# Router compares in one operation, splits moved to VectorE, first conversions and router loads moved ahead

## The chip, the cores and the metric

The kernel runs on one core of a Trainium2 chip. The core has a matrix engine (TensorE, PE in the profile, with its weight loads as PEld), VectorE (DVE), ScalarE (ACT), GpSimd (POOL) and SyncE (SP), whose queue issues the DMA transfers of this kernel. The metric is the device time of one execution in microseconds; the median of three runs is compared.

## The reference

Three layers in a row, on 2304 tokens (4 batches of 576), all in float32. Only the third one's routing is unusual: it assigns greedily over all token and expert pairs in the order of their logits, and each expert takes at most 288 tokens.

```python
# 1: block-causal attention, 4 batches x 8 heads x 576 tokens x 64
attn = softmax(where(block_i >= block_j, q @ k.T / sqrt(64), -1e9)) @ v
x = attn.transpose(0, 2, 1, 3).reshape(2304, 512)
# 2: gated feed-forward, 512 -> 1536 -> 512
h = sigmoid(x @ w_gate) * (x @ w_val)
x = h @ w_out
# 3: 8 experts, capacity 2304 // 8 = 288
logits = x @ m_gate
for idx in argsort(-logits.flatten()):
    tok, e = idx // 8, idx % 8
    if assigned[tok] >= 0 or counts[e] >= 288: continue
    assigned[tok] = e; counts[e] += 1
out[assigned == e] = maximum(x[assigned == e] @ w1[e], 0) @ w2[e]
```

## The kernel before

Matrix products keep float32 accuracy by splitting: a tensor x becomes a high part h (a rounded copy, made by ScalarE) and a low part l = x - h (made by GpSimd or VectorE), and a product is the sum of three matmuls, hh, hl and lh. Tiles whose names end in h and l are such parts.

The stages are interleaved by Python generators. Each `yield` hands over to the stage beside it, so the order of the calls of `next` is the order of the instructions on every engine, and each engine works through its own in that order. TensorE is in order too: a matmul that waits holds all behind it.

*Attention and first feed-forward* (`first_half`). Attention runs one batch ahead of the feed-forward. Before its first batch, `Ffn.start` loads the first gate and value weights, which come as 64-bit floats, converts them (`convert`, `ToF32`: one ScalarE operation, L283, and four on VectorE, L288 to L294) and splits them. `first_half` advances it once after each step of attention, from attention's fourth step on. SyncE issues loads in program order; attention's are L70 and L71, the weights' L331.

*Router weights* (`router_weights`) are worked out beside batch 1: w_out is loaded (L529), converted and multiplied with the router's gate. The first step of that generator sets tiles to zero on GpSimd, loads the gate and three tiles of w_out, and starts the first conversion.

*Second feed-forward and router.* `Ffn2.run` computes h @ w_out token tile by token tile, 18 tiles of 128 tokens: 36 matmuls of 512 columns (L660) a tile, and for the last two tiles two times 36 of 256 columns. A step of it is one wide matmul, or on average one and a half narrow ones. It is the filling work for the router. `Ffn2.split` makes the parts of the next tile of h, three chunks of 512: ScalarE L633, then GpSimd L637, then the load of the tile two on. It is advanced after every third matmul.

`Router.run` finds the greedy assignment in seven phases. A phase takes each free token's best expert (`pick`), turns that logit into an ordered key in two halves of 16 bits (`keys`), and searches for each expert's threshold in two halves of three rounds. In a round all keys are compared with 31, 63 or 64 thresholds, 18 matmuls count (L809), VectorE gives the verdict whether an expert is full (`ge`, L816), a flag matmul (L819) turns the verdicts into the new base, and VectorE compares again (L825, L830). The differences of key and threshold are made ahead by `minus` (L796), two a phase on VectorE (558 elements) and two on GpSimd (1134 and 1152), so that a round's compare needs the base alone. At a phase's end the chosen tokens get their logits lowered, and GpSimd adds them to the result (L857, L858). `FILL` says how many steps of `Ffn2.run` stand between the parts of a phase: for each half and round, ahead of the 18 matmuls and ahead of the flag matmul, and a last number ahead of the phase's last matmuls. `FIRST` and `TAIL` do so at the start and end of the router. Five tiles of expert weights are split on GpSimd meanwhile, one step of `Experts.split` with every 18 steps. After the router, `Experts.gather` fetches each expert's tokens by index.

Of the kernel before, what the change touches and what calls it, by code (L numbers as in the profile page):

```python
# [8 lines left out]
F32 = mybir.dt.float32  # L9
# [287 lines left out]
class Ffn:  # L297
# [88 lines left out]
    def start(self):  # L386

        for f in range(2):
            for j in range(2):
                self.load(0, f, j)  # L390
                yield
        for _ in range(3):
            yield
        for f in range(2):
            for j in range(2):
                for _ in self.convert(f, j):
                    yield
        for j in range(2):
            for _ in self.split(0, 0, j):
                yield  # L400
# [112 lines left out]
def router_weights(k, ffn):  # L513
# [36 lines left out]
    raws = [load(f) for f in range(3)]  # L550
    later = iter(())
# [31 lines left out]
class Ffn2:  # L583
# [40 lines left out]
    def split(self, t):  # L624
# [7 lines left out]
        for c in range(3):  # L632
            nc.scalar.activation(h[:, 4 * c:4 * c + 4], x[:, 4 * c:4 * c + 4], AF.Copy)  # L633
            yield
        for c in range(3):
            s = slice(4 * c, 4 * c + 4)
            nc.gpsimd.tensor_tensor(l[:, s], x[:, s], f32(h[:, s]), op=OP.subtract)  # L637
            yield
        self.load(t + 2)
# [8 lines left out]
    def run(self):  # L648

        k, nc = self.k, self.k.nc  # L650
        nxt = iter(())
        order = [(t, 0, 512) for t in range(16)] + [(t, c, c + 256) for c in (0, 256) for t in (16, 17)]
        for i, (t, a, b) in enumerate(order):
            h, l = self.parts[t]
            if a == 0:
                nxt = self.split(t + 1)
            o = k.psF.tile([P, 512], F32, name="A")
            for f in range(12):
                for n, (x, w) in enumerate(((h, self.oh), (h, self.ol), (l, self.oh))):
                    nc.tensor.matmul(o[:, 0:b - a], x[:, f], w[:, f, a:b], start=(f == 0 and n == 0), stop=(f == 11 and n == 2))  # L660
                    if n == 2:
                        next(nxt, None)
                    if b - a == 512 or n == 1 or f % 2:
                        yield
            drain(nxt)
# [15 lines left out]
FILL = (((13, 6), (4, 3), (6, 3)), ((8, 3), (4, 3), (6, 3)), 10)  # L681
# [4 lines left out]
class Router:  # L686
# [4 lines left out]
    def open(self, st, k):  # L691
# [63 lines left out]
        self.sub = [None, t([P, 18 * 31], F32, "sub1"), t([P, 18 * 64], F32, "sub2")]  # L755
# [35 lines left out]
    def minus(self, h, s):  # L791

        J = SEARCH[h][s][1]
        x = self.kf[:, 0 if h == 0 else 2]
        eng = self.k.nc.vector if s == 1 else self.k.nc.gpsimd
        eng.tensor_tensor(self.sub[s][:, 0:18 * J].rearrange("p (c j) -> p c j", j=J),  # L796
                                       x[:, :, None].to_broadcast([P, 18, J]),
                                       self.step[h, s][:, None, :].to_broadcast([P, 18, J]), op=OP.subtract)

    def phase(self, last):  # L800
        nc, k = self.k.nc, self.k
        v, q = nc.vector, self.q
        for h in range(2):
            base = k.psA.tile([P, 512], F32, name="A")
            for s, (sh, J) in enumerate(SEARCH[h]):
# [17 lines left out]
                if s < 2:  # L823
                    J1 = SEARCH[h][s + 1][1]
                    v.tensor_scalar(self.cmp[:, 0:18 * J1], self.sub[s + 1][:, 0:18 * J1], base[:, 0:1], None, op0=OP.is_ge)  # L825
                elif h == 0:
                    v.tensor_scalar(q[:, 0], self.kf[:, 0], base[:, 0:1], 1.0, op0=OP.subtract, op1=OP.min)
                    v.scalar_tensor_tensor(self.kf[:, 2], q[:, 0], 65536.0, self.kf[:, 1], op0=OP.mult, op1=OP.add)
                    J1 = SEARCH[1][0][1]
                    v.tensor_tensor(self.cmp[:, 0:18 * J1].rearrange("p (c j) -> p c j", j=J1),  # L830
                                    self.kf[:, 2, :, None].to_broadcast([P, 18, J1]),
                                    self.step[1, 0][:, None, :].to_broadcast([P, 18, J1]), op=OP.is_ge)

# [21 lines left out]
        if not last:  # L855
            self.pick()
# [3 lines left out]
    def run(self):  # L860
# [5 lines left out]
        for ph in range(7):  # L866
            yield from self.phase(ph == 6)
# [24 lines left out]
        hi = self.sub[1][:, 0:432].rearrange("p (c h) -> p c h", h=24)  # L892
# [22 lines left out]
class Experts:  # L915
# [27 lines left out]
    def split(self, eng):  # L943
# [16 lines left out]
        self.load()  # L960

# [155 lines left out]
def first_half(k, s1, ffn, f2, right):  # L1117
# [4 lines left out]
    while s1.done < 3:  # L1122
        next(att, None)
        if s1.step > 2:
            next(w0, None)
# [3 lines left out]
    for b in range(nb):  # L1129
# [12 lines left out]
        for c in ffn.batch(b, inline):  # L1142
# [4 lines left out]
            if b == 1:  # L1147
# [19 lines left out]
def tile_fn(ctx, tc, q, kk, v, w_gate, w_val, w_out, m_gate, w1, w2, out, dbg=None):  # L1167
# [49 lines left out]
    esp = (x for _ in range(5) for x in ex.split("g"))  # L1217
    with tc.manual_schedule():
        n = 0
# [47 lines left out]
```

## Time and profile before

| | us |
|---|---|
| median of 3 runs | 1002.01 (1000.61 to 1003.71) |
| the profiled execution | 1003.31 |
| its span, first to last instruction | 1001.5 |
| TensorE busy | 955.7 (95%) |
| VectorE busy | 552.7 (55%) |
| GpSimd busy | 475.2 (47%) |
| ScalarE busy | 425.7 (43%) |

The span is what the trace covers, and all its times count from the span's start. A busy TensorE is not a TensorE at its peak, since matmuls are pipelined and its clock has two levels. Where an engine is named after an arrow in a row, the idle time in front of the row ended when that engine's operation did. By stage: attention alone until about 75 us, feed-forward with attention until 440, feed-forward alone until 553, second feed-forward with router until 761, experts to the end.

### The profile page before, as it was taken

To read this page: it belongs to the slowest core of one execution; us is meant where nothing else is said; L and a number is where in the kernel's file an instruction comes from. 1 tells how busy PE (TensorE), PEld (TensorE's weight loads), DVE (VectorE), ACT (ScalarE), POOL (GpSimd) and SP (SyncE) were. 2 spreads that over 40 slices of the span, in tenths; PEclk is the share of its full clock that TensorE was granted. 3 is DMA by queue.
4 is the path that set the end of the run, shared out by engine and by line. 5 is a ranking of instruction groups with operands and counts; after the bars stand their busy time and mean duration, and the time that the engine had idled before them with its cause. 6 is when DMAs were issued, how large, how long until landed. Compare 5 with 4: busy or idle time off the path is not lost.

```text
span 1001.5 us, 19572 instructions
## 1 busy us (share of the span) xinstructions
PE 955.7 (95%) x7387; PEld 824.4 (82%) x7387; DVE 552.7 (55%) x1293; ACT 425.7 (43%) x998; POOL 475.2 (47%) x514
## 2 busy tenths in 40 slices
PE   6899999999999999999999988999998999999996
PEld 4568888879888988889898766666678999999996
DVE  4888888567666444441332476766651544454440
ACT  4676655445555354532431222211111555555551
POOL 2475434433434344362432777866633545445532
PEclk9899999999999999999999999999999999999998
DMA  6664667464554322225782845444323566666640
GB/s 162 173 149 133 200 190 210 132 205 167 172 176 142 111 79 90 72 83 182 263 298 84 224 124 150 142 126 113 106 85 96 189 202 188 198 202 204 199 153 24
DMA packets 191326, 155.17 MB, mean 155 GB/s; under 512 B 70785, under 2 KB 161921, under 8 KB 191233
## 3 DMA queue, kind: packets, MB, share of 16 engines
q1 hardware_dynamic: 187728, 142.92, 47.4%
q0 software_dynamic: 3504, 11.01, 3.2%
q8 instruction: 58, 0.95, 0.4%
q14 instruction: 36, 0.29, 0.1%
HBM read 116.15 MB, written 37.75 MB: 154 GB/s over the span
## 4 chain that ended last, share of the span: by engine, by line
PE 82%; DVE 10%; issue 3%; DMA 2%; POOL 1%; SPq 1%; ACT 1%; DVEq 0%; POOLq 0%; ACTq 0%
PE A L454 31%; PE A L1046 10%; PE A L1091 9%; PE A L660 9%; PE A L211 5%; PE A L163 4%; PE A L116 4%; DVE cmp L825 3%; PE A L809 2%; DVE sub L796 2%; PE A L122 2%; PE A L409 1%; PE A L85 1%; PE A L996 1%; PE A L1015 1%
## 5 line engine op out<-in xcount | busy, mean ns | idle before, releaser
L151 POOL TENSOR_SCALAR p<-p,stat 128x128 f32<-128x128 f32 (+2 forms) x144 | 80.6, 572 | 195.5 <-DVE stat L149 149.7
L454 PE MATMUL A<-xh,w1h 128*128 128x288 f32 x384 | 121.7, 317 | 2.0 <-ACT ptb L168 2.0
L454 PE MATMUL A<-xh,w0h 128*128 128x288 f32 x384 | 121.5, 316 | 0.0
L359 POOL TENSOR_TENSOR w0l<-wf,w0h 128x512 fp32r<-128x512 f32 x48 | 64.0, 1333 | 107.4 <-ACT w0h L357 104.6
L454 PE MATMUL A<-xl,w1h 128*128 128x288 f32 x384 | 113.7, 296 | 0.0
L454 PE MATMUL A<-xh,w1l 128*128 128x288 f32 x384 | 113.7, 296 | 0.0
L454 PE MATMUL A<-xl,w0h 128*128 128x288 f32 x384 | 113.2, 295 | 0.0
L454 PE MATMUL A<-xh,w0l 128*128 128x288 f32 x384 | 113.1, 295 | 0.0
L958 POOL TENSOR_TENSOR ewl<-eraw,ewh 128x512 fp32r<-128x512 f32 x56 | 74.7, 1353 | 68.2 <-ACT ewh L954 68.0
L465 DVE SCALAR_TENSOR_TENSOR h<-sg,A 128x288 f32<-128x288 f32 x96 | 43.3, 451 | 97.0 <-PE A L454 79.8
L124 DVE TENSOR_REDUCE stat<-A 128x1 f32<-128x128 f32 (+4 forms) x160 | 70.5, 478 | 46.7 <-PE A L122 28.4
L660 PE MATMUL A<-wo_h,hl 128*128 128x512 f32 (+1 forms) x240 | 94.5, 394 | 0.4 <-POOL hl L637 0.4
L464 ACT ACTIVATE sg<-A 128x288 f32<-128x288 f32 x96 | 39.3, 410 | 127.5 <-PE A L454 123.2
L660 PE MATMUL A<-wo_l,hh 128*128 128x512 f32 (+1 forms) x240 | 91.8, 383 | 0.0
L660 PE MATMUL A<-wo_h,hh 128*128 128x512 f32 (+1 forms) x240 | 90.3, 376 | 0.0
L138 ACT ACTIVATE p<-A,stat 128x128 f32<-128x128 f32 (+4 forms) x160 | 81.9, 520 | 16.1 <-DVE stat L124 13.1
L637 POOL TENSOR_TENSOR hl<-hraw,hh 128x512 fp32r<-128x512 f32 x54 | 76.1, 1437 | 22.6 <-ACT hh L633 21.6
L454 PEld LDWEIGHTS A<-xh,w1h 128*128 128x128 f32 x384 | 72.6, 189 | 10.5 <-issue 6.5
L667 ACT ACTIVATE x2r<-A 128x512 f32<-128x512 f32 (+1 forms) x20 | 11.1, 556 | 165.0 <-PE A L660 165.0
L454 PEld LDWEIGHTS A<-xh,w0h 128*128 128x128 f32 x384 | 72.3, 188 | 9.2 <-issue 5.2
L1091 PE MATMUL A<-eh,ewh 128*128 128x288 f32 x256 | 78.0, 305 | 0.0
L1046 PE MATMUL A<-exh,ewh 128*128 128x288 f32 x256 | 77.4, 302 | 0.3 <-ACT exh L999 0.3
(223 smaller groups left out, 2602.3 us busy)
## 6 DMA issues: line engine op xcount, KB each, us to landing
eraw<-in_moe_w_dram SPq DMA_DIRECT2D x64, 512.0 KB, 4.4
wf<-wgv SPq DMA_DIRECT2D x72, 256.0 KB, 3.2
h<-h SPq DMA_DIRECT2D x48, 288.0 KB, 2.4
hraw<-h SPq DMA_DIRECT2D x16, 768.0 KB, 5.8
w<-in_moe_w_gate_dram SPq DMA_DIRECT2D x12, 512.0 KB, 3.9
w<-in_moe_w_val_dram SPq DMA_DIRECT2D x12, 512.0 KB, 4.1
wgv<-wf SPq DMA_DIRECT2D x24, 256.0 KB, 3.0
w<-in_moe_w_out_dram SPq DMA_DIRECT2D x12, 512.0 KB, 4.1
```

Source lines behind the costliest of these rows:

```text
L124: nc.vector.tensor_reduce(st[:, x:x + 1], s[:, 0:w], axis=AX.X, op=OP.max, negate=True)
L138: nc.scalar.activation(o, s[:, 0:w], AF.Exp, bias=m, scale=1.0, accum_out=st[:, 2 + x:3 + x])
L151: self.k.mark = nc.gpsimd.tensor_scalar(t, t, r[:, x:x + 1], 1.0, op0=OP.mult, op1=OP.mult)
L211: nc.tensor.matmul(o[64 * a:64 * a + 64, b0:w], vs[0:kk, c, a, :], th[0:kk, a, c, b0:w], start=(n == 0), stop=(n == len(mm) - 1))
L359: nc.gpsimd.tensor_tensor(l, x, f32(h), op=OP.subtract)
L454: nc.tensor.matmul(o[:, 0:288], w[:, ks], x[:, ts], start=(kk == 0 and n == 0), stop=(kk == 3 and n == 2))
L465: nc.vector.scalar_tensor_tensor(h[:, ts], sg, 1.0, ps[1][:, 0:288], op0=OP.add, op1=OP.mult)
L637: nc.gpsimd.tensor_tensor(l[:, s], x[:, s], f32(h[:, s]), op=OP.subtract)
L660: nc.tensor.matmul(o[:, 0:b - a], x[:, f], w[:, f, a:b], start=(f == 0 and n == 0), stop=(f == 11 and n == 2))
L958: (nc.vector if eng == "v" else nc.gpsimd).tensor_tensor(l[:, s], x[:, s], f32(h[:, s]), op=OP.subtract)
L1046: nc.tensor.matmul(o[:, 0:288], w[:, s], x, start=(d == 0 and n == 0), stop=(d == 3 and n == 2))
L1091: nc.tensor.matmul(o[:, 0:288], w[:, s], x, start=(n == 0), stop=(n == 23))
```

## The change

1. *Compare in one operation.* `minus` and its tiles are gone. `at_least` subtracts the base from the key and compares the difference with the thresholds, in one VectorE operation with two tensor inputs.
2. *Splits on VectorE.* The low parts of h (54 operations) and of the first five tiles of expert weights (10) go from GpSimd to VectorE. `aside` places one of them: nine times a phase, ahead of and behind the verdict, and where the tile's three are done, it advances the expert weights (`first_splits`). What is left of a tile's splits when the tile ends is issued there. ScalarE's three copies are issued together at the tile's start.
3. *Sums on VectorE.* The two GpSimd operations at a phase's end become `closed`, in the next phase's third round.
4. *FILL.* A phase has 80 steps in place of 72.
5. *First conversions.* `Ffn.start` is advanced from attention's first step on, and its loads are spread: two behind the fifth load of attention, two behind the eighth.
6. *Router loads.* `router_weights` gives way once behind its loads, and is advanced once at step 180 (of 192) of batch 0.

```diff
@@ Ffn.start
         for f in range(2):
             for j in range(2):
                 self.load(0, f, j)
+            for _ in range((6, 3)[f]):
                 yield
-        for _ in range(3):
-            yield
@@ router_weights
     raws = [load(f) for f in range(3)]
+    yield
@@ Ffn2.split
             nc.scalar.activation(h[:, 4 * c:4 * c + 4], x[:, 4 * c:4 * c + 4], AF.Copy)
-            yield
+        yield
         for c in range(3):
             s = slice(4 * c, 4 * c + 4)
-            nc.gpsimd.tensor_tensor(l[:, s], x[:, s], f32(h[:, s]), op=OP.subtract)
+            nc.vector.tensor_tensor(l[:, s], x[:, s], f32(h[:, s]), op=OP.subtract)
+            if c == 2:
+                self.load(t + 2)
             yield
-        self.load(t + 2)
+
+    def aside(self):
+
+        if next(self.nxt, 1):
+            next(self.more, None)
...
-FILL = (((13, 6), (4, 3), (6, 3)), ((8, 3), (4, 3), (6, 3)), 10)
+FILL = (((14, 4), (5, 3), (9, 3)), ((8, 3), (5, 3), (9, 3)), 11)
@@ Router
-    def minus(self, h, s):
+    def at_least(self, h, s, x, base=0.0):
...
+        self.k.nc.vector.scalar_tensor_tensor(
+            self.cmp[:, 0:18 * J].rearrange("p (c j) -> p c j", j=J), x[:, :, None].to_broadcast([P, 18, J]), base,
+            self.step[h, s][:, None, :].to_broadcast([P, 18, J]), op0=OP.subtract, op1=OP.is_ge)
+
+    def closed(self):
+
+        v = self.k.nc.vector
+        sel = self.q[:, 4][:, None, :].to_broadcast([P, 8, 18])
+        v.tensor_tensor(self.t2, sel, self.e1[:, :, None].to_broadcast([P, 8, 18]), op=OP.mult)
+        v.tensor_tensor(self.res, self.res, self.t2, op=OP.add)
...
                 if h + s == 0:
                     self.keys()
-                if s == 0:
-                    self.minus(h, 1)
-                    self.minus(h, 2)
+                elif (h, s) != (0, 2):
+                    aside()
+                elif not first:
+                    self.closed()
                 v.tensor_scalar(self.ge[0:J], o[0:J, 0:8], CAP - 0.5, 0.0, op0=OP.is_ge, op1=OP.max,
                                 accum_out=self.fl[0:J])
+                if (h, s) != (1, 2):
+                    aside()
                 yield FILL[h][s][1]
...
                 if s < 2:
-                    J1 = SEARCH[h][s + 1][1]
-                    v.tensor_scalar(self.cmp[:, 0:18 * J1], self.sub[s + 1][:, 0:18 * J1], base[:, 0:1], None, op0=OP.is_ge)
+                    self.at_least(h, s + 1, self.kf[:, 2 * h], base[:, 0:1])
...
-        nc.gpsimd.tensor_tensor(self.t2, sel, ex, op=OP.mult)
-        nc.gpsimd.tensor_tensor(self.res, self.res, self.t2, op=OP.add)
@@ Experts
+    def first_splits(self, n):
+        cur = self.split("v")
+        next(cur)
+        yield
+        for i in range(n):
+            next(cur)
+            yield
+            nxt = self.split("v") if i < n - 1 else cur
+            if nxt is not cur:
+                next(nxt)
+            next(cur)
+            next(cur, None)
+            yield
+            cur = nxt
@@ first_half
         next(att, None)
-        if s1.step > 2:
-            next(w0, None)
+        next(w0, None)
...
-            if b == 1:
+            if b == 1 or (b, n) == (0, 180):
                 next(rw, None)
@@ tile_fn
-    esp = (x for _ in range(5) for x in ex.split("g"))
+    f2.more = ex.first_splits(5)
...
-        for w in ro.run():
+        for w in ro.run(f2.aside):
             for _ in range(w):
                 next(steps, None)
-                n += 1
-                if n % 18 == 0:
-                    next(esp, None)
         drain(steps)
-        drain(esp)
+        drain(f2.more)
```

How the instructions move. VectorE, in a phase of the router, from the last key operation to the third verdict, before (`sub` is the difference of key and threshold, `A` a PSUM bank with counts or base):

```order
L789 CAST kf<-ki 128x18
L796 TENSOR_TENSOR sub_7196<-kf,step_7147 128x558
L816 TENSOR_SCALAR ge,flag<-A 31x8
L825 TENSOR_SCALAR cmp<-sub_7196,A 128x558
L816 TENSOR_SCALAR ge,flag<-A 31x8
L825 TENSOR_SCALAR cmp<-sub_7197,A 128x1134
L816 TENSOR_SCALAR ge,flag<-A 63x8
```

The same place of the changed kernel, in a phase where the asides go to a tile of h (`hl` is the low part of h):

```order
L794 CAST kf<-ki 128x18
L827 TENSOR_SCALAR ge,flag<-A 31x8
L637 TENSOR_TENSOR hl_8387<-hraw,hh_8386 128x512
L799 SCALAR_TENSOR_TENSOR cmp<-kf,A,step_7144 128x558
L637 TENSOR_TENSOR hl_8387<-hraw,hh_8386 128x512
L827 TENSOR_SCALAR ge,flag<-A 31x8
L637 TENSOR_TENSOR hl_8387<-hraw,hh_8386 128x512
L799 SCALAR_TENSOR_TENSOR cmp<-kf,A,step_7149 128x1134
L807 TENSOR_TENSOR u_7201<-q_7204,e_7202 128x144
L808 TENSOR_TENSOR res<-res,u_7201 128x144
L827 TENSOR_SCALAR ge,flag<-A 63x8
```

The subtraction ahead of the first verdict is gone; two splits stand around the second verdict, one behind the first, and the two sums ahead of the third.

SyncE at the start, from the fifth load of attention on, before (`raw` holds q or k, `vraw` v, `w` the feed-forward's weights):

```order
L70 DMA raw<-in_k_dram 128x4x64 x2
L71 DMA raw<-in_k_dram 64x2x64
L70 DMA vraw<-in_v_dram 128x4x64 x2
L71 DMA vraw<-in_v_dram 64x2x64
L70 DMA raw<-in_q_dram 128x4x64 x2
L71 DMA raw<-in_q_dram 64x2x64
```

And of the change:

```order
L70 DMA raw<-in_k_dram 128x4x64 x2
L71 DMA raw<-in_k_dram 64x2x64
L331 DMA w_182<-in_moe_w_gate_dram 128x4x256
L331 DMA w_184<-in_moe_w_val_dram 128x4x256
L70 DMA vraw<-in_v_dram 128x4x64 x2
L71 DMA vraw<-in_v_dram 64x2x64
```

The first two weight loads stand behind five loads of attention instead of eleven.

SyncE at the turn from batch 0 to batch 1, the difference (`h_57` is batch 0's h in DRAM, `mg` the router's gate):

```order
-L319 DMA h_57<-h 128x576 x2
-L522 DMA mg<-in_moe_w_gate_dram 128x4x8
-L529 DMA w_2767<-in_moe_w_out_dram 128x1024
-L529 DMA w_2769<-in_moe_w_out_dram 128x1024
-L529 DMA w_2771<-in_moe_w_out_dram 128x1024
+L319 DMA h_57<-h 128x576
+L521 DMA mg<-in_moe_w_gate_dram 128x4x8
+L528 DMA w_2708<-in_moe_w_out_dram 128x1024
+L528 DMA w_2710<-in_moe_w_out_dram 128x1024
+L528 DMA w_2712<-in_moe_w_out_dram 128x1024
+L319 DMA h_57<-h 128x576
```

The four loads stand ahead of the last store of batch 0.

## Rows read from the trace of the kernel before

**Rows 1.** The page: busy us of each engine, share of the span, instructions.

```profile
PE 955.7 (95%) x7387; PEld 824.4 (82%) x7387; DVE 552.7 (55%) x1293; ACT 425.7 (43%) x998; POOL 475.2 (47%) x514
```

**Rows 2.** Timeline, 20.9 to 27 us: start, us, engine, operation [idle before <-releaser].

```profile
20.95 0.59 SPq L331 DMA_DIRECT2D w<-in_moe_w_gate_dram  x1
...
25.35 0.69 ACT L283 ACTIVATE cv_t<-w 128x512 f32<-128x512 f32 x1 [3.50 <-DMA w<-in_moe_w_gate_dram]
...
26.58 0.34 PE L163 MATMUL A<-ident,p 128*64 128x128 f32 x1 [1.85 <-ACT ptb L168]
```

**Rows 3.** Stretches at the lower clock: busy us by engine, PEclk, DMA.

```profile
26.60:33.50 6.90, 6.79 (x25) 2.88 (x27) 6.07 (x16) 5.11 (x16) 3.27 (x7) 0.51 0.57 178
207.50:211.00 3.50, 3.45 (x14) 3.45 (x15) 2.16 (x3) 1.76 (x7) 1.52 (x1) 0.52 0.59 226
651.40:654.80 3.40, 3.40 (x19) 2.49 (x16) 1.65 (x3) 0.00 (x0) 3.20 (x3) 0.51 0.52 155
```

**Rows 4.** Timeline, 193.5 to 208 us.

```profile
193.84 7.33 SPq L319 DMA_DIRECT2D h<-h  x2
...
205.94 0.67 ACT L283 ACTIVATE cv_t<-w 128x512 f32<-128x512 f32 x1 [6.31 <-DMA w<-in_moe_w_out_dram]
...
207.55 0.58 PE L454 MATMUL A<-xh,w1h 128*128 128x288 f32 x1 [2.04 <-ACT ptb L168]
```

**Rows 5.** Chain that ended last: start, us, what; the same operation, two phases.

```profile
688.20 1.52 DVE cmp L825
...
712.01 1.51 DVE cmp L825
```

**Rows 6.** Timeline, 601.8 to 606 us, a phase of the router.

```profile
602.02 0.52 DVE L825 TENSOR_SCALAR cmp<-sub,A 128x558 bf16<-128x558 f32 x1 [0.25 <-PE A L819]
...
602.63 0.40 PE L660 MATMUL A<-wo_l,hh 128*128 128x512 f32 x1
...
602.87 0.61 PE L809 MATMUL A<-oneh,cmp 128*128 128x8 bf16 x18
...
603.51 0.15 DVE L816 TENSOR_SCALAR_CACHE_REDUCE ge<-A 31x8 bf16<-31x8 f32 x1 [0.97 <-PE A L809]
...
604.12 0.18 PE L819 MATMUL A<-flag,wgt 128*128 128x1 bf16 x1
...
604.42 1.24 DVE L825 TENSOR_SCALAR cmp<-sub,A 128x1152 bf16<-128x1152 f32 x1 [0.75 <-PE A L819]
...
604.70 0.40 PE L660 MATMUL A<-wo_l,hh 128*128 128x512 f32 x1
...
605.40 0.40 PE L660 MATMUL A<-wo_l,hh 128*128 128x512 f32 x1
...
605.72 0.43 PE L809 MATMUL A<-oneh,cmp 128*128 128x8 bf16 x11
```

**Rows 7.** Timeline, 694 to 699 us, a later phase.

```profile
694.71 0.74 DVE L830 TENSOR_TENSOR cmp<-kf,step 128x558 bf16<-128x558 f32 x1
...
694.82 2.61 POOL L796 TENSOR_TENSOR sub<-kf,step 128x1152 f32<-128x1152 f32 x1 [1.00 <-DVE kf L828]
...
695.37 2.66 DVE L796 TENSOR_TENSOR sub<-kf,step 128x558 f32<-128x558 f32 x1
```

**Rows 8.** VectorE by line and shape, 565 to 745: busy us, mean ns.

```profile
L825 DVE TENSOR_SCALAR cmp<-sub,A 128x558 bf16<-128x558 f32 x14 | 18.7, 1334 | 7.0 <-PE A L819 7.0
```

**Rows 9.** Whole span by line and shape: busy us, mean ns, idle before.

```profile
L637 POOL TENSOR_TENSOR hl<-hraw,hh 128x512 fp32r<-128x512 f32 x54 | 76.1, 1437 | 22.6 <-ACT hh L633 21.6 <-PE A L819 0.9
...
L574 DVE TENSOR_TENSOR wol<-A,woh 128x512 fp32r<-128x512 f32 x12 | 8.3, 692 | 9.5 <-ACT woh L572 9.3
```

**Rows 10.** Timeline, 742 to 745.5 us, the router's end.

```profile
744.87 0.32 PE L905 MATMUL A<-cmp,ohlo 128*128 128x48 bf16 x6 [1.62 <-DVE ohlo L900]
```

**Rows 11.** Timeline, 755 to 763 us, the first gathers.

```profile
756.06 1.20 POOL L984 DMA_INDIRECT xg<-x2h,idx  x1 [8.86 <-DMA x2h<-x2r]
...
762.85 0.33 PE L996 MATMUL A<-ident,xg 128*128 128x128 f32 x1 [1.04 <-DMA xg<-x2h,idx]
```

More of the change, by code (lines that the diff above doesn't have):

```diff
@@ L650, in run @@
         k, nc = self.k, self.k.nc
-        nxt = iter(())
+        self.nxt = iter(())
         order = [(t, 0, 512) for t in range(16)] + [(t, c, c + 256) for c in (0, 256) for t in (16, 17)]
@@ L655, in run @@
             if a == 0:
-                nxt = self.split(t + 1)
+                self.nxt = self.split(t + 1)
+                next(self.nxt, None)
             o = k.psF.tile([P, 512], F32, name="A")
@@ L660, in run @@
                     nc.tensor.matmul(o[:, 0:b - a], x[:, f], w[:, f, a:b], start=(f == 0 and n == 0), stop=(f == 11 and n == 2))
-                    if n == 2:
-                        next(nxt, None)
                     if b - a == 512 or n == 1 or f % 2:
                         yield
-            drain(nxt)
+            drain(self.nxt)
             y = self.hb.tile([P, 512], F32, name="x2r", bufs=3)
@@ L754, in open @@
         nc.gpsimd.memset(self.cmp, 0.0)
-        self.sub = [None, t([P, 18 * 31], F32, "sub1"), t([P, 18 * 64], F32, "sub2")]
+        self.hot = t([P, 18 * 24], F32, "hot")
         self.ki = t([P, 4, 18], I32, "ki")
@@ L789, in keys, with phase @@
         v.tensor_copy(kf[:, 1], ki[:, 3])
-    def minus(self, h, s):
+    def at_least(self, h, s, x, base=0.0):
         J = SEARCH[h][s][1]
[L794 to L800, printed above, removed]
+        self.k.nc.vector.scalar_tensor_tensor(
[6 more added lines that the diff above has]
+        v.tensor_tensor(self.res, self.res, self.t2, op=OP.add)
+    def phase(self, first, aside):
         nc, k = self.k.nc, self.k
@@ L828, in phase @@
                     v.scalar_tensor_tensor(self.kf[:, 2], q[:, 0], 65536.0, self.kf[:, 1], op0=OP.mult, op1=OP.add)
[L829 to L832, printed above, removed]
+                    self.at_least(1, 0, self.kf[:, 2])
         v.scalar_tensor_tensor(self.e1, o[:, 16:24], 16.0, self.w8, op0=OP.mult, op1=OP.add)
@@ L854, in phase, with run @@
         v.scalar_tensor_tensor(k.L, sel, -BIG, k.L, op0=OP.mult, op1=OP.add)
-        if not last:
-            self.pick()
-        nc.gpsimd.tensor_tensor(self.t2, sel, ex, op=OP.mult)
-        nc.gpsimd.tensor_tensor(self.res, self.res, self.t2, op=OP.add)
-    def run(self):
+    def run(self, aside):
         nc, k = self.k.nc, self.k
@@ L866, in run @@
         for ph in range(7):
-            yield from self.phase(ph == 6)
+            if ph:
+                self.pick()
+            yield from self.phase(ph == 0, aside)
+        self.closed()
         v.tensor_scalar(self.t1, k.L, -0.1 * BIG, None, op0=OP.is_gt)
@@ L891, in run @@
         lo = self.p.tile([P, 18, P], BF16, name="ohlo")
-        hi = self.sub[1][:, 0:432].rearrange("p (c h) -> p c h", h=24)
+        hi = self.hot.rearrange("p (c h) -> p c h", h=24)
         mv = self.cmp[:, 0:864].rearrange("p (c a h) -> p c a h", a=2, h=24)
@@ L1216, in tile_fn @@
             ro.open(rst, k)
-    esp = (x for _ in range(5) for x in ex.split("g"))
+    f2.more = ex.first_splits(5)
     with tc.manual_schedule():
-        n = 0
         with tc.issue_after(k.rowed.ins):
             next(steps)
-        for w in ro.run():
+        for w in ro.run(f2.aside):
             for _ in range(w):
                 next(steps, None)
-                n += 1
-                if n % 18 == 0:
-                    next(esp, None)
         drain(steps)
-        drain(esp)
+        drain(f2.more)
     if dbg is not None:
```

## The prediction

> **What bounds the kernel now.** I read the page's busy times first, then the list of what TensorE (PE) waits for, then the chain that ended last, and then the timeline at each place where PE stood still. PE is busy for 95% of the span [rows 1], and every other engine has slack, so the time is PE's work plus PE's waits plus the stretches at the lower clock. Three places hold nearly all of it that the change touches.
>
> *The start.* SyncE issues the eleven loads of q, k and v one after the other, and the first load of FFN weights leaves only at 20.95 us. ScalarE's first conversion stands ahead of a copy that PE needs. It waits 3.50 us for that load, and PE stands 1.85 us [rows 2]. Right behind, the granted clock is 0.51 for 6.9 us [rows 3], which is the 1.2 GHz level.
>
> *The turn from batch 0 to batch 1.* SyncE holds the last store of h until h is there, from 193.84 on, for 7.33 us with the store before it, and the router's load of w_out stands behind it. ScalarE waits 6.31 us for that load with a copy for PE queued behind, and PE stands 2.04 us [rows 4]; then 3.5 us at clock 0.52 [rows 3].
>
> *The router.* One phase takes 23.81 us, by two rows one phase apart [rows 5]. What must PE do in it? A step of filling work (one matmul of 512 columns) is 0.23 us: three of them lie between 604.70 and 605.40. Between 602.63 and 604.70 lie six steps, one block of 18 compare matmuls (L809) and one flag matmul (L819), with no wait worth counting: 2.07 - 6 x 0.233 = 0.67 us for a block and its flag [rows 6]. Six of them are 4.0, with 0.2 (an estimate) for the three small matmuls at a phase's end. With 72 steps (the sums of FILL) a phase needs 72 x 0.233 + 4.2 = 21.0 us; 2.8 of 23.81 are waits, 19.6 in seven phases. Why it waits is in [rows 7]: GpSimd's subtraction takes 2.61 us, and VectorE's own one beside it takes 2.66 and holds the verdict (L816) behind it. The compare of 558 elements takes 1.33 us on average [rows 8], but 0.52 where GpSimd does not read [rows 6].
>
> **The change, part by part.**
>
> *Compare in one operation.* Both subtractions go (two on VectorE, two on GpSimd a phase), and four compares become one operation with two tensor inputs. The trace has none of that form. The nearest row is the compare of two tensors at L830, 558 elements in 0.74 us [rows 7]; beside the split of 512 in 0.69 [rows 9] that is 1.1 ns an element, so 1.39 us for 1152. I take these. Bounds: 0.52, the old form alone, below, and 1.33 for 558 (its mean today) above. On VectorE the form matters: the Trainium skill, "VectorE: DVE Perf Modes", section "Mode 2×_2P", says that an fp32 operation with one tensor in SBUF can run two elements a cycle and one with two tensors cannot, which speaks against this edit. The trace agrees in part: 0.52 against 0.74 for 558, but 1152 took 1.24 in the old form, no double rate [rows 6]. By that rule alone the two short compares grow by 0.22 us each and cost about 3 us in seven phases if PE waits for them. By the mean of their row today they shrink by 0.59 [rows 8]. The sum goes by the durations of the rows and by the walk below.
>
> *GpSimd leaves the router stage.* Its 54 splits of h, 10 of expert weights and the two sums a phase go to VectorE. A split costs 0.69 on VectorE against 1.44 on GpSimd [rows 9]; 0.69 is from a row with one input in PSUM, and I take it, with 1.44 as the upper bound.
>
> *Do the splits fit?* The walk, with the latencies of [rows 6]: the verdict can start 0.64 us after its block (602.87 to 603.51) and takes 0.15; the flag matmul comes 1.25 after the block with three steps between; 0.30 later a compare can start; 0.06 after its end the next block can. So between the end of one compare and the start of the next VectorE has 0.06 + 1.25 + 0.30 = 1.61 us, and two splits and the verdict need 1.53. They fit, with nothing to spare. After the flag matmul the chain is 0.30 + 0.74 + 0.06 = 1.10 us against 5 steps (1.17), and 0.30 + 1.39 + 0.06 = 1.75 against 9 (2.10). What misses: in two phases a tile of h ends outside the gaps and its remaining splits stand in a row (ahead of the key operations, or of a verdict), 0.6 us late each. I leave 2.0 us of waits in seven phases, between 0.5 and 10 (10 with the compare at 1.33).
>
> *FILL.* 72 steps a phase become 80. The work only moves: the 56 steps no longer stand behind the router. A phase without waits is 80 x 0.233 + 4.2 = 22.8 us. **Router: 19.6 - 2.0 = 17.6 us gained.** The drop to 0.51 at 651.4 [rows 3] lies in this stage; without the waits ahead of it I count it gone, 3.4 x 0.5 = 1.7.
>
> *Costs around the router.* The first three splits of h stand on VectorE behind the last gate of the batch: 0.4 (estimate; bounds 0 and 2, three splits at 0.69). The router's end: PE waits up to 1.62 us there today for the one-hot rows [rows 10]; the same 35 steps now cover half-width matmuls, some 1.7 us less, and three splits (2.1) stand ahead of the chain, while GpSimd no longer disturbs VectorE. 0.6 worse (bounds: 1.6 better, 3.5 worse). Behind the router 35 instead of 91 steps are left, about 6 us. The index goes through gathers from 756.06 to PE's 762.85, 6.8 us, which today wait for the x2 store and not for the index, with 1.04 us of wait left on PE [rows 11]; now both come together: 0.4 worse.
>
> *First conversions sooner.* Weight loads follow the fifth load of attention, so the first leaves near 10 us instead of 20.95, and lands near 14.4 at the same 4.4 us. In ScalarE's order the conversion now stands ahead of the first copy of transposed probabilities, for which I estimate 16 us. The 1.85 us go; of the 6.9 us at 0.51, which cost 3.4, I count 2.9, since VectorE is busy 6.07 of those 6.90 and may be next. SyncE's later loads of v, q and k move by 1.2 us (two issues of 0.59); conversions now stand among attention's first small operations on VectorE, 0.7 back (an estimate, about one such operation). **Start: 1.85 + 2.9 - 0.7 = 4.0**, bounds 0 (the loads collide) and 5.2.
>
> *Router loads sooner.* At step 180 of batch 0 the w_out loads are issued ahead of the held store, so at about 194 instead of 201.7; 4.3 us of landing end near 199, before the conversion. VectorE's two small operations on the gate wait for their own load with one product of the batch behind them, which no PE work waits for. **2.04 + 3.5 x 0.48 = 3.7**, bounds 2 and 3.9.
>
> **Sum:** 17.6 + 1.7 - 0.4 - 0.6 - 0.4 + 4.0 + 3.7 = 25.6 us. The profiled execution took 1003.31 us with a span of 1001.5, and the median of the three runs is 1002.01, 1.3 below it; 1001.5 becomes 975.9, and the median 976.4: 976.
>
> **The rivals.**
> *The compare stays slow.* If 1.33 is what such a compare costs with a PSUM operand, GpSimd or not, PE waits 0.5 to 0.6 us at two or three places a phase, about 10 us. The row of 0.52 speaks against it. 976 + 8 = 984. Chance 0.12.
> *The start gives nothing.* 1 MB of weights ahead of v, q and k makes attention late by what was won; PE's list would show raw loads where ScalarE stood. 980. Chance 0.15.
> *Everything fits better.* No waits are left in the router, start at its upper bound: 976 - 2 - 1.2 - 1.5 = 971. Chance 0.10.
> *VectorE becomes the bound, and the kernel slower.* Place: the gaps around the verdict. They hold two splits up to 0.73 us each, with the spare of the longer fills about 0.81; what is above goes into PE's wait, once for each of some 55 splits. At GpSimd's 1.44 that is 55 x 0.63 = 35 us against 27.6 won (the sum without its 2.0): 1009. It turns slower from 0.81 + 27.6/55 = 1.31 us a split. Against it stands 0.69, with no GpSimd work left to collide with. Chance 0.03.
> *The change doesn't do what it says*: the waits only move, because the phase is bound by VectorE's round trips. The walk speaks against it; start and w_out loads would gain their lower bounds, 2 to 4 us. 999, chance 0.03.
>
> **How the numbers follow.** The forecast (972 to 981 alone) holds 0.57, the rivals the rest. The range that leaves out 2 in 10 at most goes from 969 (start and router at their better bounds) to 986 (slow compare, start half lost). A difference under 0.3%, 3 us, is what a measurement here cannot tell from no change; so same is 999 to 1005: 0.02. Faster 0.95, slower 0.03.
>
> **What would show it.** Right: no subtraction rows; compares near 0.74 and 1.39; splits near 0.7; phase period 22.8 to 23.2; no clock 0.5 stretch near 26, 207 and 651; PE's waits for the verdict under 2 us in all. Wrong: PE waiting for a split of h, compares above 1, a new wait on raw loads in the first 30 us, or a dip of the clock that moved instead of going.

## The result, and the profile after

The changed kernel takes 975.0 us (974.5 to 976.2, four runs) against 1002.2 for the kernel before: ratio 0.9731, 95% interval 0.9713 to 0.9748. Forecast were 976.0, between 969 and 986. The profiled execution took 976.2 with a span of 974.5, 27.0 less than the span before.

The page's busy line of the changed kernel; compare [rows 1]:

```profile
PE 946.3 (97%) x7387; PEld 822.4 (84%) x7387; DVE 557.6 (57%) x1357; ACT 425.9 (44%) x998; POOL 339.0 (35%) x422
```

The matmuls are the same 7387, and PE's share rises from 95 to 97%: what was won is waiting and clock.

Where on the way was it won? Below, matmuls by line and output: first and last start of the feed-forward's, the second feed-forward's, and the one that ends each router phase.

```profile
L453 PE MATMUL A<-xh,w0h x384: 288/295/512, 72.7 to 543.8; 128*128 128x288 f32 x192
L667 PE MATMUL A<-wo_h,hh x240: 281/391/504, 545.8 to 733.3; 128*128 128x512 f32 x96, 128*128 128x256 f32 x24
L857 PE MATMUL A<-row,ones x7: 177/177/178, 578.8 to 715.6; 128*128 128x1 bf16 x7
```

Before:

```profile
L454 PE MATMUL A<-xh,w0h x384: 288/295/512, 75.2 to 551.0; 128*128 128x288 f32 x192
L660 PE MATMUL A<-wo_h,hh x240: 277/389/628, 553.0 to 761.1; 128*128 128x512 f32 x96, 128*128 128x256 f32 x24
L848 PE MATMUL A<-row,ones x7: 177/177/177, 584.9 to 730.5; 128*128 128x1 bf16 x7
```

So 2.4 us are won at the start, 4.8 more at the turn of batch 0 to 1 (the lead is 7.2 when the second feed-forward begins) and 20.5 in that stage with the router. 27.7 are won when the first expert product starts (736.0 against 763.7), and 0.7 is lost after. These starts are called the stage's marks below. Six phases take (715.6 - 578.8) / 6 = 22.80 us each, with 80 steps; before, 24.27 with 72.

VectorE's costliest groups in the router, 556 to 745 us; compare [rows 8, 9]:

```profile
L637 DVE TENSOR_TENSOR hl<-hraw,hh 128x512 fp32r<-128x512 f32 x51 | 34.3, 681 | 4.9 <-ACT hh L633 4.8
L799 DVE SCALAR_TENSOR_TENSOR cmp<-kf,A,step 128x558 bf16<-128x558 f32 x14 | 11.2, 800 | 2.5 <-PE A L832 2.1
L799 DVE SCALAR_TENSOR_TENSOR cmp<-kf,A,step 128x1152 bf16<-128x1152 f32 x7 | 10.0, 1424 | 2.2 <-PE A L832 2.0
...
L966 DVE TENSOR_TENSOR ewl<-eraw,ewh 128x512 fp32r<-128x512 f32 x10 | 6.8, 681 | 0.0
```

No subtraction is left, a split costs 0.68, and the new compare 0.80 for 558 elements (0.74 without the PSUM operand) and 1.42 for 1152. What PE still waits for, 545 to 745 us: us in total, times, longest.

```profile
PE A L1019 <- DMA xg<-x2h,idx: 2.1, 2, 1.1
PE A L832 <- DVE ge L827: 1.4, 3, 0.5
PE A L667 <- DVE hl L637: 1.2, 2, 0.8
PE A L913 <- DVE ohlo L908: 0.9, 2, 0.5
...
```

Before, 556 to 740 us:

```profile
PE A L819 <- DVE ge L816: 6.5, 7, 1.2
PE A L809 <- DVE cmp L825: 6.2, 12, 0.7
PE A L809 <- DVE oneh L778: 1.7, 2, 0.8
```

The verdict (`ge`) is late three times, 1.4 us in all, each time behind a split at a tile's start, which itself waits for ScalarE's copy (1.66 us at 621.34). The compares, 6.2 us before, are not in the list any more. The list falls by 13.0 us in the phases, which is less than the 20.5 of the stage: PE's busy time in the stage, for the same matmuls, falls by 6.3 (191.8 to 185.5 us up to the first expert product). Up to 1.7 of that is the stretch at half clock; the rest, as far as is known, is waits that the list doesn't show because the ends of matmuls are modelled. The three windows of [rows 3] and a new one (PEclk is the third number from the end):

```profile
26.60:33.50 6.90, 6.42 (x45) 3.69 (x44) 6.73 (x20) 4.71 (x15) 3.70 (x8) 1.00 0.67 199
207.50:211.00 3.50, 3.50 (x27) 3.03 (x28) 3.38 (x9) 2.18 (x6) 0.99 (x3) 1.00 0.79 286
651.40:654.80 3.40, 3.40 (x48) 2.59 (x47) 3.25 (x12) 2.02 (x4) 0.00 (x0) 1.00 0.29 64
744.50:747.90 3.40, 3.40 (x17) 3.40 (x16) 0.92 (x2) 1.64 (x3) 0.00 (x0) 0.50 0.28 107
```

The old three are at full clock; the last, behind the waits for the two gathers, is at 0.50 for 3.4 us and costs up to 1.7. That it is what is lost behind the router is not shown: a second execution of this kernel, traced later, has such a stretch too and takes 237.2 us from the first expert product to the end, against 238.5 here and 237.8 before.

At the start the first conversion no longer waits (first row: no idle time ahead of it; compare [rows 2]), but at 54.34 PE waits 1.36 us, where before it waited 0.57 (at 56.49):

```profile
16.77 0.67 ACT L283 ACTIVATE cv_t<-w 128x512 f32<-128x512 f32 x1
...
52.30 1.26 POOL L359 TENSOR_TENSOR w1l<-wf,w1h 128x512 fp32r<-128x512 f32 x1
52.31 1.27 DVE L146 TENSOR_SCALAR stat<-stat 128x2 f32<-128x2 f32 x1
...
53.54 1.09 POOL L151 TENSOR_SCALAR p<-p,stat 128x576 f32<-128x576 f32 x2
...
54.34 0.33 PE L163 MATMUL A<-ident,p 128*128 128x128 f32 x1 [1.36 <-POOL p L151]
```

GpSimd's split of the first weights (`w1l`) and VectorE's operation on two elements a partition start together, and the small one, 0.16 us at most of its other places, takes 1.27. Then GpSimd comes to `p`, for which PE waits. This pair of rows is what the experiments turned out to be about. The trace before has such a pair as well:

```profile
56.39 1.28 POOL L359 TENSOR_TENSOR w0l<-wf,w0h 128x512 fp32r<-128x512 f32 x1
56.41 1.29 DVE L146 TENSOR_SCALAR stat<-stat 128x2 f32<-128x2 f32 x1
```

### The profile page after: what moved, and what is told of

It reads as the page before. It is cut to its first block, busy times and chain, and to the rows that moved or that the text cites. A ratio compares the mean times of both kernels' runs of the same rounds, so it can differ in the third digit from the quotient of the medians.

```text
span 974.5 us, 19511 instructions
## 1 busy us (share of the span) xinstructions
PE 946.3 (97%) x7387; PEld 822.4 (84%) x7387; DVE 557.6 (57%) x1357; ACT 425.9 (44%) x998; POOL 339.0 (35%) x422
## 4 chain that ended last, share of the span: by engine, by line
PE 89%; DVE 4%; issue 2%; POOL 1%; DMA 1%; SPq 1%; ACT 1%; POOLq 0%; ACTq 0%; DVEq 0%
PE A L453 32%; PE A L667 15%; PE A L1069 10%; PE A L1114 9%; PE A L211 5%; PE A L116 4%; PE A L163 4%; PE A L819 2%; PE A L122 2%; PE A L408 1%; PE A L85 1%; PE A L1019 1%; PE A L1038 1%; DVE stat L124 1%; PE A L535 1%
## 5 line engine op out<-in xcount | busy, mean ns | idle before, releaser
L667 PE MATMUL A<-wo_h,hl 128*128 128x512 f32 (+1 forms) x240 | 91.8, 383 | 1.2 <-DVE hl L637 1.2
L966 POOL TENSOR_TENSOR ewl<-eraw,ewh 128x512 fp32r<-128x512 f32 x46 | 58.9, 1303 | 69.0 <-ACT ewh L962 64.8
L966 DVE TENSOR_TENSOR ewl<-eraw,ewh 128x512 fp32r<-128x512 f32 x82 | 60.5, 738 | 29.1 <-ACT ewh L962 29.1
L1069 PE MATMUL A<-exl,ewh 128*128 128x288 f32 x256 | 76.3, 298 | 0.2
```

Source lines behind the costliest of these rows:

```text
L966: (nc.vector if eng == "v" else nc.gpsimd).tensor_tensor(l[:, s], x[:, s], f32(h[:, s]), op=OP.subtract)
L1069: nc.tensor.matmul(o[:, 0:288], w[:, s], x, start=(d == 0 and n == 0), stop=(d == 3 and n == 2))
```

## The experiments

Theory: the compares and verdicts were late because VectorE and GpSimd worked on tensors in SBUF at the same time; so both halves of the router's change are needed, the compare in one operation and the splits on VectorE. Rivals: one of the two does it all; the new FILL does it; the new form of the compare is itself the better or the worse one.

### One half of the router's change at a time

*Splits back on GpSimd.* In `Ffn2.split` and `first_splits`:

```diff
-            nc.vector.tensor_tensor(l[:, s], x[:, s], f32(h[:, s]), op=OP.subtract)
+            nc.gpsimd.tensor_tensor(l[:, s], x[:, s], f32(h[:, s]), op=OP.subtract)
-        cur = self.split("v")
+        cur = self.split("g")
```

> The changed kernel with the splits of h and of the five tiles of expert weights back on GpSimd at the same places of the program; the compare stays one operation. Theory (GpSimd's reading beside VectorE is what made the compares slow, by 0.52 to 1.33 us): the compare of 558 elements rises from 0.80 to between 1.2 and 1.6 us on average, PE waits again in most rounds, and the time is 985, between 981 and 995. Rival (GpSimd was harmless, only the subtractions held the chain): compares stay at 0.8, time between 974 and 977.

Measured 1004.6 us (ratio 1.0027, 1.0008 to 1.0047): the rival is out, but it is 20 us above the theory's figure and 10 above its range. The compare of 558 elements took 1.05 on average, less than expected, so the compares are not all. VectorE and GpSimd from 580.6 us:

```profile
580.59 0.74 DVE L780 TENSOR_TENSOR cmp<-val,grid 128x558 bf16<-128x558 f32 x1
...
580.60 4.41 POOL L637 TENSOR_TENSOR hl<-hraw,hh 128x512 fp32r<-128x512 f32 x3 [3.37 <-ACT hh L633]
...
581.24 1.42 DVE L783 TENSOR_TENSOR oneh<-logits,val 128x144 bf16<-128x144 f32 x1
...
582.58 1.23 DVE L789 TENSOR_SCALAR ki<-val 128x18 int32<-128x18 int32 x1
...
583.85 1.20 DVE L790 TENSOR_TENSOR ki<-val,ki 128x18 int32<-128x18 int32 x1
...
584.97 1.26 POOL L966 TENSOR_TENSOR ewl<-eraw,ewh 128x512 fp32r<-128x512 f32 x1
...
585.08 1.19 DVE L791 TENSOR_SCALAR ki<-ki 128x18 int32<-128x18 int32 x1
586.18 0.16 DVE L792 TENSOR_SCALAR ki<-ki 128x18 int32<-128x18 int32 x1
586.30 0.18 DVE L793 TENSOR_SCALAR kf<-ki 128x18 f32<-128x18 int32 x1
```

`ki` is an operation on 18 elements a partition: 0.17 us at 586.18, but 1.23, 1.20 and 1.19 beside GpSimd's splits, about the time of one split. Its delay does not go with its own size; by these rows each such operation waits out one split and then runs. So a split on GpSimd costs not a share of the compare's time but up to 1.2 us for an operation of any size in the chain. What PE waits for, 556 to 740 us:

```profile
PE A L819 <- DVE cmp L799: 8.5, 8, 2.3
PE A L832 <- DVE ge L827: 5.5, 3, 2.3
PE A L819 <- DVE oneh L783: 4.3, 3, 2.0
PE A L857 <- DVE q L851: 1.0, 1, 1.0
```

The longest are 2.3 us. With them four stretches at half clock, 17.0 us in all, lie in this kernel's router, against none in the changed kernel's. Not every operation of VectorE is held; three rows of this kernel, 558 to 745 us, most of them beside a split:

```profile
L840 DVE SCALAR_TENSOR_TENSOR kf<-q,kf 128x18 f32<-128x18 f32 x7 | 4.3, 619 | 0.2
L827 DVE TENSOR_SCALAR_CACHE_REDUCE ge<-A 31x8 bf16<-31x8 f32 x28 | 4.3, 153 | 26.6 <-PE A L819 26.6
...
L848 DVE TENSOR_REDUCE q<-t 128x18 f32<-128x144 f32 x7 | 2.1, 303 | 0.2
```

In the changed kernel these take 178, 153 and 303 ns.

*Subtractions back, splits on VectorE.* `minus` as before, called where it was, and

```diff
-                    self.at_least(h, s + 1, self.kf[:, 2 * h], base[:, 0:1])
+                    v.tensor_scalar(self.cmp[:, 0:18 * J1], self.sub[s + 1][:, 0:18 * J1], base[:, 0:1], None, op0=OP.is_ge)
```

> The changed kernel with the subtractions back (two on VectorE and two on GpSimd a phase, at their old places) and the compare in its old form; the splits stay on VectorE. Theory (the subtractions beside each other hold the verdict): VectorE's subtraction takes 2 us or more beside GpSimd's, the verdict behind it is late twice a phase, the time is 990, between 982 and 1000. Rival (the form with one tensor input is the faster one, and without GpSimd's splits nothing disturbs it): compares of 558 at 0.52, time 975 or up to 3 us less. Second rival (only the splits on GpSimd mattered): 974 to 977.

Measured 993.7 (0.9914, 0.9892 to 0.9936), a time inside the theory's range. The reason that it gave is only half of it. VectorE, 558 to 745 us:

```profile
L637 DVE TENSOR_TENSOR hl<-hraw,hh 128x512 fp32r<-128x512 f32 x48 | 51.3, 1076 | 4.8 <-ACT hh L633 4.7
L802 DVE TENSOR_TENSOR sub<-kf,step 128x558 f32<-128x558 f32 x14 | 12.2, 872 | 0.0
...
L851 DVE TENSOR_SCALAR cmp<-sub,A 128x558 bf16<-128x558 f32 x14 | 7.1, 508 | 0.3 <-PE A L845 0.3
L851 DVE TENSOR_SCALAR cmp<-sub,A 128x1152 bf16<-128x1152 f32 x7 | 5.8, 825 | 2.8 <-PE A L845 2.2
```

The subtraction on VectorE takes 0.87 on average, not 2 or more; what GpSimd's two subtractions of 2.6 us now hold up is mostly the splits, 1.08 instead of 0.68. And the old form is the faster one when it is let alone, 0.51 and 0.83: the first rival had the row right and the time wrong.

*Neither half, start and loads only* (the kernel before with points 5 and 6 of the change):

> The kernel before with the edits of the start and of the router loads alone; router, splits, sums and FILL as before. By the prediction's two terms 4.0 + 3.7 = 7.7 us faster: 994.3. By the stage marks (7.2 won by the end of batch 1): 994.9. With the two runs that put back one half of the router's change (compare in one operation with splits on GpSimd 1004.6, splits on VectorE with subtractions 993.7) this closes a square: if the two halves simply add, the gain of both, 975.0, would be the sum of the single ones, which 994.9 - 1004.6 = -9.7 and 994.9 - 993.7 = 1.2 are far from.

Measured 996.0 (0.9948, 0.9928 to 0.9968), 1 to 2 us above both figures. The square:

| us | splits on GpSimd | splits on VectorE |
|---|---|---|
| subtractions and compare | 996.0 | 993.7 |
| compare in one operation | 1004.6 | 975.0 |

(The upper left one has FILL, sums and the places of the splits as before, the others the new ones. So +8.6 below is the price of the compare in one operation together with these; splits on GpSimd at their old places beside the new compare were not tried, nor the sums alone.) The single halves bring +8.6 and -2.3, both together -21.0. The intervals of 996.0 and 993.7 overlap, so the -2.3 is not clear of noise, but the sum of the halves is far from -21.0. They don't add.

*Subtractions back, all four on VectorE:*

```diff
-        eng = self.k.nc.vector if s == 1 else self.k.nc.gpsimd
-        eng.tensor_tensor(self.sub[s][:, 0:18 * J].rearrange("p (c j) -> p c j", j=J),
+        self.k.nc.vector.tensor_tensor(self.sub[s][:, 0:18 * J].rearrange("p (c j) -> p c j", j=J),
```

> The changed kernel with the subtractions back, all four of a phase on VectorE at their old places, and the compare in its old form; GpSimd has nothing left in the router. Theory (what slows VectorE beside GpSimd is that one waits for the other, whatever its own size; the run with two of the four subtractions on GpSimd shows splits of 1.08 us on average for 0.68): splits at 0.68 and subtractions at 0.74 and 1.4, compares at 0.51 and 0.82, and the verdict behind the subtractions is late by 0.74 + 1.40 - 0.5 of slack = 1.6 us twice a phase, 23 us, less what the shorter compares do not give: 990 to 998. Rival (VectorE's added work hardly matters once GpSimd is silent): 975 to 982.

Measured 992.4 (0.9904, 0.9874 to 0.9934), inside the theory's range. VectorE and PE's longest wait, 558 to 745 us:

```profile
L637 DVE TENSOR_TENSOR hl<-hraw,hh 128x512 fp32r<-128x512 f32 x48 | 32.3, 679 | 5.9 <-ACT hh L633 5.8
L801 DVE TENSOR_TENSOR sub<-kf,step 128x558 f32<-128x558 f32 x14 | 10.3, 737 | 0.0
...
L850 DVE TENSOR_SCALAR cmp<-sub,A 128x558 bf16<-128x558 f32 x14 | 7.0, 500 | 0.3 <-PE A L844 0.3
...
L850 DVE TENSOR_SCALAR cmp<-sub,A 128x1152 bf16<-128x1152 f32 x7 | 5.8, 825 | 3.6 <-PE A L844 3.3
```
```profile
PE A L844 <- DVE ge L839: 13.2, 14, 2.5
...
```

With GpSimd silent every operation has its own time, and the splits are back at 0.68. Yet PE waits 13.2 us for the verdict, twice a phase: the subtractions stand ahead of it. Two stretches at half clock (3.4 us each) lie in this router too. So there were two causes that each suffice: GpSimd beside VectorE, and VectorE's own subtraction in front of the verdict. The change takes away both.

### How near VectorE is to being the bound

```diff
+            for _ in range(2):
                 nc.vector.tensor_tensor(l[:, s], x[:, s], f32(h[:, s]), op=OP.subtract)
```

> The changed kernel with every split of h on VectorE issued twice (the second writes the same values), so 1.38 us instead of 0.69 at each aside. By the arithmetic of the rival in the prediction (gaps around the verdict hold two splits up to 0.81 us each, what is above goes into PE's wait, once for each of some 55 splits): 55 x (1.38 - 0.81) = 31 us, 1006. Rival (the slack read from the changed kernel's trace, 0.45 us ahead of a flag matmul and 0.25 or 0.55 ahead of a block of compare matmuls, takes up part of it, and a split behind the compare costs nothing): 12 to 22 us, 987 to 997.

Measured 999.0 (0.9961, 0.9942 to 0.9979), between the two and outside both. 24.0 us over 54 splits is 0.44 for each 0.69 added, so a split of up to 1.38 - 0.44 = 0.94 us would cost nothing by this straight line, where the prediction had 0.81. Two stretches at half clock lie in its router and two behind it (3.4 us each), against one behind the changed kernel's, so the bare waits cost less than 24.0, and 0.94 is an estimate.

### The start and the loads alone

*Start as before* (point 5 undone). 

> The changed kernel with the start as before. By the prediction's term for the start it gives back 4.0 us: 975.0 + 4.0 = 979.0. By the stage marks of the two traces (first matmul of the feed-forward at 75.16 before and 72.74 after) it gives back 2.4: 977.4, with that matmul near 75.2, ScalarE's wait of 3.5 us and a stretch of clock 0.5 near 26. By the rival that the start gives nothing it stays at 975 and later stages take back what is won.

Measured 978.1 (0.9747, 0.9723 to 0.9772): 3.1 back by the medians, though this interval overlaps the changed kernel's. In the trace ScalarE waits 4.64 us for the weights and PE 2.98, until 27.93; a stretch at half clock of 6.8 us begins at 27.4, still inside that wait; the first feed-forward matmul starts at 76.1.

*Loads as before* (point 6 undone). 

> The changed kernel with the router loads where they were. By the prediction's term it gives back 3.7 us: 978.7. By the stage marks (lead over the kernel before 2.4 us at the end of batch 0, 7.2 in batch 1) it gives back 4.8: 979.8, with PE waiting about 2 us for the copies of transposed probabilities near 203, about 0.9 for attention's scores ahead of that, and a stretch of clock 0.5 behind it. By the rival that the waits only move it stays at 975.

Measured 979.1 (0.9761, 0.974 to 0.9782): 4.1 back; its four runs (978.1 to 979.7) all lie above the changed kernel's (974.5 to 976.2). PE's rows with idle time ahead, 200 to 206 us:

```profile
201.73 0.48 PE L116 MATMUL A<-kf,qf 64*128 64x256 f32 x1 [0.21 <-DVE ptb L170]
...
205.27 0.42 PE L453 MATMUL A<-xh,w1h 128*128 128x288 f32 x1 [2.22 <-ACT ptb L168]
```

By the last feed-forward matmul 4.9 are lost (548.7 for 543.8): the 2.22, the half of a stretch at half clock (3.4 us at 205.5), and 0.9 at the scores (L116), by the starts of the feed-forward's matmuls around them; the row shows 0.21 of it, since ends are modelled. VectorE's first operation on the router's gate waits 2.43 us for its load at 200.80, with the copy `ptb` behind it that the scores wait for. This trace has one more stretch at half clock, 21.2 to 24.6 us, and the first feed-forward matmul starts at 72.7 all the same.

### FILL, and a faster version

*FILL as before* (72 steps). 

> The changed kernel with the FILL of before, 72 steps a phase instead of 80. By the walk of the prediction the compares miss their blocks by 0.17 and 0.35 us twice a phase, 1.0 us a phase, 7 us, of which the 56 steps moved behind the router cover 1.0 to 2.7 (the wait for the gather, and a stretch of clock 0.5 behind it): 980. By the slack read from the changed kernel's trace (0.24 and 0.56 us ahead of the blocks, of which the shorter fills take 0.23 and 0.70) 0.3 us a phase, 2 us, so that it comes to 974.5, between 973 and 977. Rival (the new FILL is what brought the gain): above 983.

Measured 976.7 (0.9746, 0.9715 to 0.9778). The slack was there (compares end 0.06 us ahead of four of the six blocks of a phase, just in time), but the 56 steps moved behind the router did not cover the gathers (PE waits 3.2 us for them instead of 2.1). By the medians FILL carries 1.7 us of the gain; the intervals overlap, so it may be nothing.

*FILL in step with the tiles:*

```diff
-FILL = (((14, 4), (5, 3), (9, 3)), ((8, 3), (5, 3), (9, 3)), 11)
+FILL = (((11, 3), (5, 3), (8, 3)), ((7, 3), (5, 3), (8, 3)), 10)
```

> The changed kernel with FILL = (((11, 3), (5, 3), (8, 3)), ((7, 3), (5, 3), (8, 3)), 10), 72 steps a phase, taken where the changed kernel's trace shows slack ahead of the blocks. 72 steps are two tiles of h, so the tiles end at the same two places in each phase, and no splits should be left to stand in a row ahead of a verdict. Theory: no waits in the router (1.4 us won), 56 steps more behind it cover the first gather (1.0), and the stretch of clock 0.5 near 744 may go (1.7): 971.5, between 970.5 and 973. Rival (the slots have no slack to give, each step less is a wait): 7 x 8 x 0.233 = 13 us of cover gone, 980 or more.

Measured 975.0 (0.9732, 0.9701 to 0.9764): no gain, where the theory said 970.5 to 973. PE's whole list from 545 to 745 us is now

```profile
PE A L1019 <- DMA xg<-x2h,idx: 2.8, 2, 1.7
PE A L667 <- DVE hl L637: 1.6, 2, 0.8
PE A L1069 <- ACT exh L1022: 0.3, 2, 0.2
```

The theory's signs are there: no wait in the seven phases (the two for `hl` stand ahead of the first and behind the last), and no stretch at half clock before the program's end. But the gathers wait 2.8 instead of 2.1, although the index is worked out 10 us sooner (matmul L913 at 717 instead of 727): they wait for the last rows of x2. And the second feed-forward, which begins 0.4 us later in this execution, ends where it did (733.4): of some 1.9 us of waits won in it 0.3 shows in its length (187.2 for 187.5), and where the rest went stays open.

*The same, with two edits at waits that are left:*

```diff
@@ Ffn.start
         for j in range(2):
+            for _ in range((0, 4)[j]):
+                yield
             for _ in self.split(0, 0, j):
@@ Router.run
-        yield TAIL[0]
+        yield TAIL[0] - 5
+        for _ in range(3):
+            aside()
+        yield 5
```

> The kernel with FILL in step with the tiles (72 steps a phase), and two edits at the waits that its trace still shows: the three splits of tile 16 of h stand behind the router's last phase instead of in a row at the end of tile 15 (0.82 us of PE's wait), and at the start the second split of the first FFN weights on GpSimd comes four steps later, behind attention's last product on GpSimd (PE's wait of 1.35 us near 53). By the trace 2.2 us less than the run with FILL alone: 972.8, first matmul of the feed-forward 1.3 earlier. Rival for the start (VectorE is full from 20 to 53 us, so the wait comes back behind another operation): that matmul stays at its place, and the time is 974.2.

> The changed kernel once more, for the comparison with the run beside it: 975.0, between 974.3 and 976.3. The stretch of clock 0.5 near 744 is missing in three kernels with the same or longer waits at the gathers; if it is fixed by what TensorE does there, it shows again, if not, it may be absent.

Measured 973.35 (0.9718, 0.9695 to 0.9741), and 975.0 (0.9735, 0.9713 to 0.9757) for the changed kernel beside it. The two intervals overlap, so by the times alone this is 1.7 us in the right direction and no more; in the traces the first expert product starts at 734.0 against 736.0, and the first feed-forward matmul at 71.4 against 72.7. The wait near 53 is gone, as said; of the 0.82 in the router's tail 0.55 came back as a wait for the one-hot rows. The changed kernel shows a stretch at half clock behind the router again, but not at the same place: it lies at 737.4 to 740.8, behind the first gather, and the stretch near 744 is at full clock.

## Why the prediction was right, and where it was off

The total was 1.0 us off the median; the terms were further off and made up for each other, so that the total came so near is luck.

- *Router, forecast 17.6 + 1.7 - 0.4 - 0.6 = 18.3; by the stage's marks 20.5.* The mechanism held: the verdict no longer stands behind a subtraction, and GpSimd has no work left in the phases. The period of 23.81 us, read from two rows one phase apart, was the shortest kind of phase; the mean of six was 24.27, one of them (25.25) with the stretch at half clock. Waits that are left are 1.4 us and not 2.0, and for another reason: not the splits in a row at a tile's end, but the next tile's first split, which waits for ScalarE. The 1.7 for the stretch at 651.4 was counted as gone with the waits ahead of it. The run with start and loads only has the router of before and its waits (6.4 for the verdict, 6.2 for the compares, the longest 1.2) and no such stretch; the same phase takes 23.98 there, 1.27 less. So the stretch cost about 1.3, and that the router's change is what removed it is not shown. The router's end, forecast 0.6 worse, has 0.9 us of waits for the one-hot rows instead of 2.1, and 0.45 for a split at 718.86. The phase without waits was well worked out: 22.8 forecast and 22.80 measured (0.14 of it waits); FILL in step with the tiles gives (704.2 - 576.8) / 6 = 21.23 with 72 steps, where the sum gives 21.0.
- *Costs of the operations.* 0.74 and 1.39 were taken, 0.80 and 1.42 measured, 0.69 and 0.68 for a split. The walk's gap, two splits and a verdict in 1.61 us, holds.
- *The step on the form of the compare failed* ("1152 took 1.24 in the old form, no double rate"). The prediction set 1.24 us for 1152 elements in the old form against the rule of the Trainium skill ("VectorE: DVE Perf Modes", section "Mode 2×_2P"). That row [rows 6] ran beside GpSimd's split, and its 1.24 is not the operation's own. Alone it takes 0.83, and from 558 to 1152 elements (825 - 500) / 594 = 0.55 ns an element, against (1424 - 800) / 594 = 1.05 in the new form. So the form has its double rate in these rows, as the rule says. The edit pays in spite of it, because the compare in its slot had slack and the subtraction in front of the verdict had none.
- *Why the halves don't add.* The prediction treated GpSimd as slowing a neighbour (1.33 for 0.52). The rows show something harder, an operation of 0.17 us that takes 1.2. The Trainium skill says as much ("SBUF — State Buffer", section "SBUF: two separate sides"): the two engines share a pair of ports, which the one that starts first holds for its whole instruction, against VectorE operations with two SBUF inputs or in a two-port mode. The trace agrees: the reduction (0.30) and the verdict, which reads PSUM (0.15), keep their times beside a split, while `ki`, `oneh`, `kf` and the compares wait for up to one split. In which mode an operation ran no row shows.
- *Start, forecast 4.0; 3.1 by the run without it, 2.4 to 3.4 by the marks.* The wait of 1.85 and the stretch at 0.51 are gone, as worked out; their price and the 0.7 for what is put behind them were not right. From 20 to 48 us VectorE is busy 27.4 of 28 us, and the conversions that came sooner met attention's own operations and GpSimd's splits (the row at 52.31, where PE's wait grew by 0.8). Beside so full a VectorE a stretch at the lower clock need not cost what it takes from PE: the one at 21.2 in the run with the loads undone did not move the first feed-forward matmul. How the difference splits between the 2.9 for the clock and the 0.7 stays open.
- *Loads, forecast 3.7, bounds 2 to 3.9; 4.1 by the run, 4.8 by the marks.* The prediction followed VectorE's operations on the gate in the changed kernel, where no PE work waits for them, and not in the kernel before, where the scores did: 0.9.
- *Gather, forecast -0.4; -0.7 after the router.* PE waits 1.03 us for the first gather, as before. A stretch at half clock behind it was named only as a sign of error. It shows in two executions of the changed kernel, at two places, and not in those with FILL in step, with waits as long, so what decides it stays open; and by the two executions (238.5 and 237.2 us from the first expert product on) the -0.7 is within what one kernel varies.

## What to carry to other kernels

An off-path engine's duration is not its price: look at small operations of the neighbour that take as long as one of its own, and count those as one wait each. Here one stood in the trace before, at 56.41, where it cost little. Before a row is used as an operation's own cost, see what ran beside it. When two edits remove two causes of which each suffices, price them together, and test each alone before one is thrown away.

## What the runs showed that was not expected

- A VectorE operation on 18 elements: 0.17 us alone, 1.19 to 1.23 beside GpSimd's split of 512.
- One half of a change that saves 21 us, the compare in one operation with the splits left on GpSimd, costs 8.6 by itself.
- Waits do not by themselves bring the lower clock: the run with subtractions back on both engines had 17 us of waits in the router (the longest 1.4) and no stretch below full clock before the program's end, the one with splits on GpSimd 19 us (the longest 2.3) and four; and the router of before has its stretch at 651.4 in its own trace and none in the run with start and loads only, with the same waits.
